# A new order of work, with all k products and w_out casts on GpSimd, in a fused linear-attention and maxout kernel

## The chip, the cores and the metric

The kernel runs on one core of one Trainium2 chip. A core has a matrix engine (TensorE, PE in the profile), three engines for elementwise work (VectorE or DVE, ScalarE or ACT, GpSimd or POOL), and a queue engine (SyncE, SP) that issues loads. Time is the device time of one execution in microseconds; the number for a kernel is the median of several runs.

## The reference

Two parts follow each other. The first is a recurrent linear attention with a decay per key channel, for 4 batches, 8 heads, 768 steps and head size 48:

```python
for t in range(S):
    state = alpha[:, :, t, :, None] * state + np.einsum('bhd,bhe->bhde', k[:, :, t], v[:, :, t])
    y[:, :, t] = np.einsum('bhd,bhde->bhe', q[:, :, t], state)
```

The result, as x of 3072 tokens by 384, goes through a maxout layer with 1024 hidden channels:

```python
h1 = x @ w1
h2 = x @ w2
g = np.maximum(h1, h2)
return (g @ w_out).astype(np.float32)
```

All inputs and the output are 32-bit floats in memory.

## The kernel before

**The mathematics as the kernel has it.** The recurrence is cut into chunks of 128 steps. In a chunk, the decay is a running sum of logarithms. ScalarE takes the logarithm of alpha (`lg`, L481), TensorE forms the running sums by a product with a triangle of ones (`cs`, L492, or L503 for the first units), and ScalarE takes exp of the sums and of their negatives (`em`, L530 and L532). k is multiplied by `em` (`kn`, L573) and q by the exponential of the sums (`qn`, L575). Both are transposed on TensorE (`tp`, L583) and copied out of PSUM (`qu` or `qk`, L588 and L593). TensorE forms the scores k times q (`pp`, L676); VectorE masks them with a triangle (`pt`, L698); y is the masked scores times v plus q times the old state (`y`, L707 and L710). The state is carried as `tm` and `sb` (L659 to L663, L634), with k times v from TensorE (`kv`, L604 or L647). y is cast (`yc`, L718), transposed (`x`, L724) and copied to `xt` (L732 and L735).

The maximum of two products is rewritten: max(h1, h2) = relu(x(w1 - w2)) + x w2. So the kernel forms w12 = w1 - w2 (L460, VectorE, in four pieces) and w2o = w2 w_out (L440 transposes of w2, L450 products, L454 copies), both once. For a unit it computes relu(x w12) (`hp` and `gt`, L765 and L776) and then x w2o + relu(...) w_out (`op`, L796), copies it out of PSUM (`os`, L804) and stores it. All products take 16-bit operands. w_out is cast to 16 bits (`wo16`, L465) in four pieces of 128 x 768; a piece holds two of the eight blocks of 128 hidden channels, and every one of the three L450 sums needs all eight.

**Units.** A unit is 256 steps of one batch, two chunks; there are 12 units, unit u being batch u mod 4, and steps 256 (u div 4) onward. The function `gla` records the first part of a unit and `moe` the second, `weights` and `w2_rows` the work on the weights. Units 0 to 2 hold their steps in an interleaved layout (`TWO`), the others in plain order.

**What sets the order.** Nothing is executed when it is recorded. `Plan.add` records an operation with its engine, an estimated length in us, what it reads and writes, and a key. `Plan.schedule` then lays all operations on the engines by simulating them: at each moment an engine takes, of the operations that are ready and whose PSUM banks are free, the one with the lowest key. Keys are 10 times the unit plus an offset; `PRI` adds to single operations' keys, and `KEY_...`, `JOIN_...` to kinds of them. The order that results is then emitted, each engine running its own part in that order. The estimated lengths have no effect on the chip but through that order. Where TensorE has a gap of over 0.15 us in the first 40 us of the plan, products of a zero tile (`wsrc`, L471) are emitted as filler. A group that uses a part of TensorE's rows (L492, L604, L676) is marked `tiled`, and has its own key (`join`) when the group before it was tiled as well.

**Loads.** SyncE issues all loads. `HEAD` gives their order at the start: a, k, q, v with a number are the four inputs of that unit, w2 and w1 with a number are thirds and quarters of w2 and w1, wo with a number are quarters of w_out (the four pieces). From unit 2 on the loads follow unit by unit.

Of the kernel before, what the change touches and what calls it, by code (L numbers as in the profile page):

```python
# [184 lines left out]


KEY_W12 = 8
KEY_W = 3
KEY_WO = 21
KEY_M = 20  # L190
CAPS = {'g': 6, 'm': 5, 'w': 3}
W12_POOL = ()
WT_ACT = (0,)
WO_ACT = (2, 3)
RELU_DVE = 99
TM_ACT = 2
X_LAST = 0
LATER = 0.75
# [2 lines left out]
TWO = (0, 1, 2)  # L201
MERGE = 3
COMBO = 99
JOIN_CS = -2
JOIN_PP = -50
CS_UP = 2
RING = 3
PAIR = 2
PAIR_ON = 'DVE'
W2_ON = ('A', 'A', 'P')  # L210
XT_ACT = ()
QU_ACT = (1,)
KN_DVE = (0,)
VX_DVE = (0,)
PRI = {'PE:op.1.1.0@1': 10, 'PE:op.0.0.0@0': 15.0, 'PE:op.1.0.0@1': 3, 'PE:op.0.1.0@0': 4.5, 'DVE:tm.4.1@3': -33.5, "POOL:('vx', 2).1@2": -16.5, 'PE:hp.1.1@1': -3.0, 'PE:cs.4.0@4': -10, 'POOL:kn.1@6': -5, 'POOL:sb.0.0@4': 12, 'PE:hp.3.3@3': 1.5, 'ACT:qu.0.1@0': -13.5, 'PE:hp.4.1@4': 5.0, 'DVE:pt.1.1@5': 5, 'PE:pp.0.1.0@0': -15, 'DVE:pt.0.0@0': 9, 'PE:y.5.0@5': 10.5, 'PE:hp.5.1@5': 13.5, 'DVE:tm.2.1@3': -9, 'ACT:cs.7.0@7': 5, 'PE:op.4.1.0@4': 9, 'DVE:tm.2.1@4': -11, 'PE:y.0.0@0': 5, 'DVE:pt.0.1@3': 10, 'PE:cs.2.0@2': -9, 'DVE:tm.3.1@5': 9, 'ACT:cs.7.1@7': -5, 'PE:hp.2.3@2': -3, 'PE:pp.1.0.0@1': 3}
HEAD = 'a0 a1 k0 q0 v0 q1 k1 w20 w22 v1 w21 wo0 wo1 wo2 w13 w10 wo3 w11 w12'


@with_exitstack
def kernel(  # L220
# [51 lines left out]
    GT = sbt("gt", [128, NF, 2 * C], FP16, 3)  # L272
    OS = sbt("os", [128, 2, DM], FP32, 3)
    VX = sbt("vx", [128, 3, H, D], FP16, max(1, len(TWO)))
    QU = sbt("qu", [128, 2, 2, HP, 2, 64], FP16, 2)
    w2f, w1f = (LD[i].rearrange("p a x -> p (a x)").rearrange("p (s f) -> p s f", s=ND) for i in (4, 5))
    wof = LD[6].rearrange("p a x -> p (a x)").rearrange("p (s d) -> p s d", s=NF)
    w2h, = sbt("w2h", [128, ND, DFF], FP16)
# [15 lines left out]

    def two(t):
        return t.rearrange("p (h r d) -> p r h d", r=2, h=H)

    P = Plan()
    P.pri, P.u = PRI, None
# [8 lines left out]
    def b16(x, n):  # L308
        return bank(x)[:, :].bitcast(FP16)[:, 0:n]
# [65 lines left out]
        )  # L375
    add("POOL", c_u, 0.6, writes=["u16"], key=KEY_T2)
    for i in range(RING):
        add("DVE", lambda i=i: nc.vector.memset(KN[i][:, :, D:64], 0.0), 0.17, writes=[("kn", i)], key=-6)
        add("DVE", lambda i=i: nc.vector.memset(QN[i][:, :, D:64], 0.0), 0.17, writes=[("qn", i)], key=-5)
    for i in range(2):  # L380
        add("DVE", lambda i=i: nc.vector.memset(LS[i][:, :, D:64], 0.0), 0.17, writes=[("ls", i)], key=KEY_T2)
    for i in range(4):
# [74 lines left out]
    def weights(g):  # L457
        fs = slice(256 * g, 256 * g + 256)
        eng, ns = ("POOL", nc.gpsimd) if g in W12_POOL else ("DVE", nc.vector)
        add(eng, lambda: ns.tensor_sub(out=w12[:, :, fs], in0=w1f[:, :, fs], in1=w2f[:, :, fs]),  # L460
            1.9 if g in W12_POOL else 0.95, reads=[("w1f", g), *(("w2f", ds) for ds in range(ND))],
            writes=[("w12", g)], key=KEY_W12)
        on = g in WO_ACT
        cp = nc.scalar.copy if on else nc.gpsimd.tensor_copy
        add("ACT" if on else "POOL", lambda: cp(  # L465
            out=wo16[:, 2 * g : 2 * g + 2, :], in_=wof[:, 2 * g : 2 * g + 2, :]),
            0.73 if on else 0.9, reads=[("wof", g)], writes=[("wo16", g)], key=KEY_W)

    def busy(n, b):
        for _ in range(n):  # L470
# [67 lines left out]
    def gla(u):  # L538
        P.u = u
        n, by2 = u % NLD, u in TWO  # L540
        k0 = 10 * u
        de, cp = DE[u % 8], u // B
        if u == 0 or u - 1 < max(COMBO, MERGE):
# [20 lines left out]
        def prep(i):  # L564
            ci = 2 * u + i
            kk, m3 = k0 + 2 + 2.5 * i, ci % RING
            kn, qn = KN[m3], QN[m3]
            kin = two(KF[n])[:, i] if by2 else nat(KF[n])[:, i]
            qin = two(QF[n])[:, i] if by2 else nat(QF[n])[:, i]
            rk = [("kf", n, x) for x in ((0, 1) if by2 else (i,))]  # L570
            rq = [("qf", n, x) for x in ((0, 1) if by2 else (i,))]
            on, ns = ("DVE", nc.vector) if ci in KN_DVE else ("POOL", nc.gpsimd)
            add(on, lambda: ns.tensor_mul(out=kn[:, :, 0:D], in0=kin, in1=EM[m3]),  # L573
                0.55 if on == "DVE" else 0.97, reads=[*rk, ("em", m3)], writes=[("kn", m3)], key=kk)
            add("DVE", lambda: nc.vector.tensor_mul(out=qn[:, :, 0:D], in0=qin, in1=csv(u, i)),  # L575
                0.5, reads=[*rq, ("cs", u, i)], writes=[("qn", m3)], key=kk)
            tp = ("tp", u, i)
            P.ps(tp, 1, "g")
            for w, (src, key) in enumerate(((qn, ("qn", m3)), (kn, ("kn", m3)))):
                def e_tp(w=w, src=src):  # L580
                    t = b16(tp, 1024).rearrange("p (w j c) -> p w j c", w=2, j=HP)
                    for j in range(HP):
                        nc.tensor.transpose(t[:, w, j, :], pm(src[:, 2 * j : 2 * j + 2, :]), ident)  # L583
                add("PE", e_tp, 0.222, reads=[key, "ident"], writes=[tp], key=kk)
            if by2:
                on = ci in QU_ACT
                cp = nc.scalar.copy if on else nc.vector.tensor_copy
                add("ACT" if on else "DVE", lambda: cp(  # L588
                    out=qu[:, :, :, :, i, :].rearrange("p a w j c -> p (w j) a c"),
                    in_=b16(tp, 1024).rearrange("p (y a c) -> p y a c", a=2, c=64)),  # L590
                    1.0 if on else 0.65, reads=[tp], writes=[("qu", TWO.index(u) % 2, i)], key=kk)
            else:
                add("DVE", lambda: nc.vector.tensor_copy(  # L593
                    out=QK[m3], in_=b16(tp, 1024).rearrange("p (w j c) -> p w j c", w=2, j=HP)),
                    0.6, reads=[tp], writes=[("qk", m3)], key=kk)
                add("POOL", lambda: nc.gpsimd.tensor_copy(out=VC[ci % 4], in_=nat(VF[n])[:, i]),  # L596
                    0.48, reads=[("vf", n, i)], writes=[("vc", ci % 4)], key=kk)
# [12 lines left out]
        def chunk(a):  # L610
# [5 lines left out]
            for x in (kvp, yp, xp, *pp):  # L616
                P.ps(x, 1, "g")
            if by2:
                qt = [qu[:, a, w].rearrange("p j r c -> p j (r c)") for w in range(2)]
                rqk, vc, rv, um, ru = [("qu", TWO.index(u) % 2, 0), ("qu", TWO.index(u) % 2, 1)], vx[:, 2 * a], [(vk, x) for x in range(4)], u2, "u2"  # L620
            else:
                qt = [QK[m3][:, w] for w in range(2)]
                rqk, vc, rv, um, ru = [("qk", m3)], VC[m4], [("vc", m4)], u16, "u16"
# [14 lines left out]
            if more:  # L638
                if by2:
                    if a == 0:  # L640
                        P.ps(("kv", u, 1), 1, "g")
                        add("PE", kv2, 0.35, reads=[("kn", (2 * u) % RING), ("kn", (2 * u + 1) % RING), (vk, 0), (vk, 1)],
                            writes=[("kv", u, 0), ("kv", u, 1)], key=kk + 0.1, tiled=True)
                else:
                    def e_kv():
                        for j in range(HP):
                            nc.tensor.matmul(  # L647
                                b32(kvp, DM)[:, 96 * j : 96 * j + 96], lhsT=pm(KN[m3][:, 2 * j : 2 * j + 2, :]),
                                rhs=pm(vc[:, 2 * j : 2 * j + 2, :]), start=True, stop=True,
                            )  # L650
                    add("PE", e_kv, 0.168, reads=[("kn", m3), ("vc", m4)], writes=[kvp], key=kk + 0.1)
                tmi = P.tm_next(u % B)
                for h2 in range(2):
                    r, e = slice(64 * h2, 64 * h2 + 64), slice(D * h2, D * h2 + D)
# [12 lines left out]

            qts[a] = (qt, pp, rqk)

            def e_p(which):  # L670
                for w in which:
                    qt, pp, _ = qts[w]
                    for j in range(HP):
                        for e in range(2):
                            r = slice(64 * e, 64 * e + D)
                            nc.tensor.matmul(b32(pp[e], 512)[:, C * j : C * j + C], lhsT=qt[1][r, j, :],  # L676
                                             rhs=qt[0][r, j, :], start=True, stop=True)
            if u < MERGE:
                add("PE", lambda: e_p((a,)), 0.215, reads=rqk, writes=pp, key=kk, tiled=True, join=kk + JOIN_PP)
            elif a == 0:  # L680
                for x in (("pp", u, 1, 0), ("pp", u, 1, 1)):
                    P.ps(x, 1, "g")
# [11 lines left out]
                else:  # L694
                    add("PE", lambda: e_p((0, 1)), 0.43, reads=rd, writes=wr, key=k0 + 4.5, tiled=True, join=k0 + 4.5 + JOIN_PP)
            uv = um.rearrange("p r c -> p (r c)") if by2 else um
            for e in range(2):
                add("DVE", lambda e=e: nc.vector.tensor_mul(  # L698
                    out=pt[:, e], in0=b32(pp[e], 512).rearrange("p (j c) -> p j c", j=HP),
                    in1=uv.unsqueeze(1).to_broadcast([128, HP, C])),  # L700
                    0.6, reads=[pp[e], ru], writes=[("pt", m3, e)], key=kk)

            def e_y():
                t = b32(yp, DM)
# [7 lines left out]
                            start=not has, stop=(e == 1) or not has,  # L712
                        )
            add("PE", e_y, 0.378 if has else 0.21,
                reads=[*rqk, ("pt", m3, 0), ("pt", m3, 1), *rv] + ([("sb", m4, 0), ("sb", m4, 1)] if has else []),
                writes=[yp], key=kk)
            yc = YC[ci % 2]
            add("ACT", lambda: nc.scalar.copy(out=yc, in_=b32(yp, DM)),  # L718
# [171 lines left out]
```

## Time and profile before

| | us |
|---|---|
| median of 8 runs | 138.03 (137.86 to 138.21) |
| the profiled execution | 138.12 |
| span of the profiled execution | 136.4 |

The span reaches from the first instruction of the program to the end of the last. Busy time of the engines and what TensorE's time is made of, by the page:

| engine or group | busy us | share or count |
|---|---|---|
| TensorE | 130.9 | 96% |
| VectorE | 91.0 | 67% |
| ScalarE | 91.0 | 67% |
| GpSimd | 65.4 | 48% |
| filler on TensorE (L471) | 10.4 | 122 products |
| k products on GpSimd (L573) | 22.7 | 23, mean 1000 ns |
| relu on ScalarE (L776) | 28.3 | 48, mean 599 ns |

In a row for a group the line comes first, then engine, operation, what is written and read, the shapes, and the count; then busy time, the mean length of one in ns, and how long the engine idled just before these and what released it. Products on TensorE are pipelined: the length of one is about twice the interval at which they follow each other, so the interval is what counts. In the chain of waits each row is a start, a length, and an engine with a line.

### The profile page before, as it was taken

Reading aid. Unit: us, or ns where it says so; the run is one execution under the profiler, and the core shown is the slowest. Engines: PE = TensorE matmul, PEld = TensorE weight load, DVE = VectorE, ACT = ScalarE, POOL = GpSimd, SP = SyncE. Lnnn points to the kernel's source line nnn. Section 1 sums busy time; section 2 is a strip of 40 time slices with the busy share of each in tenths; the row PEclk is TensorE's granted clock in tenths of the full one; section 3 lists DMA queues with packets and bytes.
Section 4 is the critical chain, followed back from the end, with each engine's and each line's share of the span. In section 5 each row is a group of like instructions: output and inputs, shape, how many; then the busy total and the mean of one; then the engine's idle time right before and its main releaser. Section 6 shows DMA issues by size and latency. Waiting matters only on the chain.

```text
span 136.4 us, 4240 instructions
## 1 busy us (share of the span) xinstructions
PE 130.9 (96%) x1669; PEld 101.6 (75%) x1669; DVE 91.0 (67%) x201; ACT 91.0 (67%) x189; POOL 65.4 (48%) x126
## 2 busy tenths in 40 slices
PE   6999799999999999999999999999999999999990
PEld 6888676777668777777877778777778778777870
DVE  4589797823899878967789489566758657572000
ACT  3695785899856957865846667568749468264640
POOL 7464874007593484470780873743747619300000
PEclk9999999999999999999999999999999999999999
DMA  4999999999999999989999989999999030030202
GB/s 98 325 327 386 390 366 358 292 247 265 213 210 241 249 217 251 276 163 191 285 184 248 280 190 265 243 233 262 213 194 244 6 115 0 5 115 0 107 26 103
DMA packets 84179, 28.58 MB, mean 210 GB/s; under 512 B 78400, under 2 KB 83392, under 8 KB 84160
## 3 DMA queue, kind: packets, MB, share of 16 engines
q1 hardware_dynamic: 81120, 23.60, 72.3%
q10 hardware_dynamic: 3040, 4.72, 9.4%
q8 instruction: 13, 0.21, 0.6%
q14 instruction: 6, 0.05, 0.1%
HBM read 23.59 MB, written 4.72 MB: 208 GB/s over the span
## 4 chain that ended last, share of the span: by engine, by line
PE 81%; SPq 9%; DMA 6%; ACT 1%; issue 1%; ACTq 0%
PE pb L796 31%; PE pb L765 23%; PE pb L583 7%; DMA ld<-in_moe_w_out_dram 6%; SPq L393 5%; PE pb L676 4%; SPq L421 3%; PE pb L710 3%; PE pb L724 3%; PE pb L707 2%; PE pb L492 2%; PE pb L450 2%; PE pb L647 2%; PE pb L525 1%; ACT wo L465 1%
## 5 line engine op out<-in xcount | busy, mean ns | idle before, releaser
L573 POOL TENSOR_TENSOR kn<-ld,em 128x384 f16<-128x384 f32 x23 | 22.7, 1000 | 34.9 <-ACT em L530 27.3
L796 PE MATMUL pb<-wo,gt 128*128 128x384 f16 (+2 forms) x200 | 39.2, 319 | 0.0
L765 PE MATMUL pb<-xt,w 128*128 128x256 f16 x288 | 35.6, 272 | 0.0
L776 ACT ACTIVATE gt<-pb 128x512 f16<-128x512 f32 x48 | 28.3, 599 | 8.5 <-PE pb L765 7.6
L698 DVE TENSOR_TENSOR pt<-pb,u 128x512 f16<-128x512 f32 x48 | 30.0, 682 | 5.9 <-PE pb L676 5.4
L765 PEld LDWEIGHTS <-w 128*128 128x128 f16 x288 | 27.0, 98 | 4.4 <-issue 0.6
L634 POOL TENSOR_TENSOR sb<-tm,dd 64x192 f16<-64x192 f32 x40 | 20.2, 506 | 10.7 <-DVE tm L659 5.2
L796 PEld LDWEIGHTS <-gt 128*128 128x128 f16 x200 | 17.4, 98 | 8.2 <-issue 0.3
L804 ACT COPY os<-pb 128x384 f32<-128x384 f32 (+2 forms) x25 | 11.7, 466 | 16.5 <-PE pb L796 16.5
L593 DVE COPY qk<-pb 128x1024 f16<-128x1024 f16 x18 | 12.4, 689 | 7.3 <-PE pb L583 7.1
L575 DVE TENSOR_TENSOR qn<-ld,pb 128x384 f16<-128x384 f32 x24 | 12.5, 548 | 6.7 <-ACT pb L532 4.9
L796 PE MATMUL pb<-w2o,xt 128*128 128x384 f16 (+2 forms) x75 | 15.8, 319 | 0.0
L718 ACT CAST yc<-pb 128x384 f16<-128x384 f32 x24 | 11.7, 489 | 5.4 <-PE pb L710 5.4
L530 ACT ACTIVATE em<-pb 128x384 f32<-128x384 f32 x24 | 11.1, 488 | 3.6 <-PE pb L492 2.6
L659 DVE TENSOR_TENSOR tm<-pb,sb 64x192 f32<-64x192 f32 x32 | 11.3, 352 | 0.9 <-PE pb L647 0.2
L481 ACT ACTIVATE lg<-ld 128x768 f16<-128x768 f32 x12 | 10.1, 845 | 2.5 <-DMA ld<-in_alpha_dram 2.4
L471 PE MATMUL pb<-wsrc 128*128 128x128 f16 x122 | 10.4, 243 | 1.1 <-DVE wsrc L313 1.1
L532 ACT ACTIVATE pb<-pb 128x384 f32<-128x384 f32 x24 | 11.0, 486 | 0.0
L710 PEld LDWEIGHTS <-pt 128*128 128x128 f16 x192 | 9.7, 96 | 1.3
L596 POOL CAST vc<-ld 128x384 f16<-128x384 f32 x18 | 9.2, 509 | 1.9 <-DMA ld<-in_v_dram 1.3
L735 DVE COPY xt<-pb 128x384 f16<-128x384 f16 x18 | 6.3, 353 | 5.2 <-PE pb L724 4.7
L471 PEld LDWEIGHTS <-wsrc 128*128 128x128 f16 x122 | 8.8, 111 | 1.1 <-DVE wsrc L313 1.0
(86 smaller groups left out, 182.4 us busy)
## 6 DMA issues: line engine op xcount, KB each, us to landing
ld<-in_alpha_dram SPq DMA_DIRECT2D x12, 384.0 KB, 4.7
out_dram<-os ACTq DMA_DIRECT2D x11, 384.0 KB, 3.5
ld<-in_k_dram SPq DMA_DIRECT2D x18, 192.0 KB, 4.6
ld<-in_q_dram SPq DMA_DIRECT2D x18, 192.0 KB, 4.4
ld<-in_v_dram SPq DMA_DIRECT2D x18, 192.0 KB, 4.5
ld<-in_moe_w_dram SPq DMA_DIRECT2D x3, 512.0 KB, 6.6
ld<-in_moe_w_out_dram SPq DMA_DIRECT2D x4, 384.0 KB, 7.9
ld<-in_moe_w_dram SPq DMA_DIRECT2D x4, 384.0 KB, 8.7
```

The costliest lines, as they stand in the source:

```text
L471: nc.tensor.matmul(PB[b][:, 0:128], lhsT=wsrc, rhs=wsrc, start=True, stop=True)
L573: add(on, lambda: ns.tensor_mul(out=kn[:, :, 0:D], in0=kin, in1=EM[m3]), 0.55 if on == "DVE" else 0.97, reads=[*rk, ("em", m3)], writes=[( ...
L575: add("DVE", lambda: nc.vector.tensor_mul(out=qn[:, :, 0:D], in0=qin, in1=csv(u, i)), 0.5, reads=[*rq, ("cs", u, i)], writes=[("qn", m3)], ...
L593: add("DVE", lambda: nc.vector.tensor_copy(out=QK[m3], in_=b16(tp, 1024).rearrange("p (w j c) -> p w j c", w=2, j=HP)), 0.6, reads=[tp], w ...
L634: add("POOL", lambda r=r, e=e: nc.gpsimd.tensor_mul(out=sb[r, :, e], in0=TM[tmo][r], in1=dd[r, :].unsqueeze(2).to_broadcast([64, HP, D])), ...
L698: add("DVE", lambda e=e: nc.vector.tensor_mul(out=pt[:, e], in0=b32(pp[e], 512).rearrange("p (j c) -> p j c", j=HP), in1=uv.unsqueeze(1).t ...
L710: nc.tensor.matmul(t[:, 96 * j + D * e : 96 * j + D * e + D], lhsT=pt[:, e, j, :], rhs=vc[:, 2 * j + e, :], start=not has, stop=(e == 1) o ...
L718: add("ACT", lambda: nc.scalar.copy(out=yc, in_=b32(yp, DM)), 0.38, reads=[yp], writes=[("yc", ci % 2)], key=kk)
L765: nc.tensor.matmul(t[:, m, :], lhsT=w12[:, ds, f * 128 : f * 128 + 128], rhs=xt[:, ds].rearrange("p a c -> p (a c)"), start=(ds == 0), sto ...
L776: add("ACT", lambda g2=g2, v2=v2: nc.scalar.activation(out=g2, in_=v2(), func=ACTF.Relu), 0.48, reads=[x], writes=[("gt", u % 3, f2)], key ...
L796: nc.tensor.matmul(b32(x, c1 - c0), lhsT=l, rhs=r, start=first and y == 0, stop=last and y == len(ws) - 1)
L804: add("ACT", lambda m=m, x=x, c0=c0, c1=c1: nc.scalar.copy(out=os_[:, m, c0:c1], in_=b32(x, c1 - c0)), 0.06 + w / 1200.0, reads=[x], write ...
```

## The change

Constants, estimated lengths and placements change, and with them the order on all engines.

- All four casts of w_out go to GpSimd (`WO_ACT` is empty; pieces 3 and 4 were on ScalarE).
- All 24 k products go to GpSimd (`KN_DVE` is empty; chunk 0's was on VectorE).
- The copy of transposed x of chunk 1 goes from VectorE to ScalarE (`XT_ACT`).
- The relu of the second pair of hidden blocks goes from ScalarE to VectorE for units 2 to 11 (`RELU_DVE`).
- In `HEAD`, k of unit 0 now precedes alpha of unit 1, v of unit 0 precedes q of unit 0, and the last piece of w_out precedes the first piece of w1 that stood before it.
- Keys, `JOIN_CS` and the whole table `PRI` are new. The lengths assumed for the casts of w_out are 0.83 and 0.85 (were 0.73 and 0.9), that of a k product on VectorE 1.0 (was 0.55).
- Operations on a chunk can be cut into two halves by head (`HALF`). `HALF` is empty, so none is cut; the names by which operations depend on each other now carry the half.
- The tile `qu` and the transposes for it are stored with q and k next to each other for each pair of heads; sizes and counts stay.

```diff
-KEY_W = 3
-KEY_WO = 21
-KEY_M = 20
+KEY_W = 9
+KEY_WO = 16
+KEY_M = 18
...
-WO_ACT = (2, 3)
-RELU_DVE = 99
+WO_ACT = ()
+RELU_DVE = 2
...
-JOIN_CS = -2
+JOIN_CS = -5
...
-XT_ACT = ()
+XT_ACT = (1,)
 QU_ACT = (1,)
-KN_DVE = (0,)
+HALF = ()
+KN_DVE = ()
...
-HEAD = 'a0 a1 k0 q0 v0 q1 k1 w20 w22 v1 w21 wo0 wo1 wo2 w13 w10 wo3 w11 w12'
+HEAD = 'a0 k0 a1 v0 q0 q1 k1 w20 w22 v1 w21 wo0 wo1 wo2 w13 wo3 w10 w11 w12'
...
-    QU = sbt("qu", [128, 2, 2, HP, 2, 64], FP16, 2)
+    QU = sbt("qu", [128, 2, HP, 2, 2, 64], FP16, 2)
...
-            0.73 if on else 0.9, reads=[("wof", g)], writes=[("wo16", g)], key=KEY_W)
+            0.83 if on else 0.85, reads=[("wof", g)], writes=[("wo16", g)], key=KEY_W)
...
-            add(on, lambda: ns.tensor_mul(out=kn[:, :, 0:D], in0=kin, in1=EM[m3]),
-                0.55 if on == "DVE" else 0.97, reads=[*rk, ("em", m3)], writes=[("kn", m3)], key=kk)
...
+                add(on, lambda hs=hs: ns.tensor_mul(out=kn[:, hs, 0:D], in0=kin[:, hs], in1=EM[m3][:, hs]),
+                    0.53 if nh == 2 else 1.0 if on == "DVE" else 0.97,
+                    reads=[*rk, ("em", m3)], writes=ks, key=kk)
...
+                        t = t.rearrange("p (j w c) -> p w j c", w=2, j=HP) if by2 else t.rearrange("p (w j c) -> p w j c", w=2, j=HP)
...
-                qt = [qu[:, a, w].rearrange("p j r c -> p j (r c)") for w in range(2)]
+                qt = [qu[:, a, :, w].rearrange("p j r c -> p j (r c)") for w in range(2)]
```

What the new order is around the steps that matter: before, TensorE's products with pieces 1 and 2 of w_out (L450) had y of unit 1's first chunk between them, and six products with piece 4 came after two L765 groups; now y comes after the first products with piece 2, and the six come after one L765 group. On GpSimd the casts are pieces 1, 2, half of `sb` of unit 1, piece 3, the other half, piece 4. The scores of unit 3 and the sums of unit 4 stood next to each other, and now have three L765 groups between them. The relu on VectorE stands ahead of the masks of the next unit (L698).

## The prediction

> **What bounds the kernel now.** I read the page's busy shares first, then the waits, then the chain of waits, and last the timeline where the chain leaves TensorE.
>
> ```profile
> PE 130.9 (96%) x1669; PEld 101.6 (75%) x1669; DVE 91.0 (67%) x201; ACT 91.0 (67%) x189; POOL 65.4 (48%) x126
> ...
> L471 PE MATMUL pb<-wsrc 128*128 128x128 f16 x122 | 10.4, 243 | 1.1 <-DVE wsrc L313 1.1
> ```
>
> TensorE is busy nearly all the time, and 10.4 us of that is filler (L471, multiplying zeros while data is on the way). The list of TensorE's own waits holds one row between 18 and 28 us, and is empty from 22.1 to 133 us:
>
> ```profile
> PE pb L450 <- POOL wo L465: 0.3, 1, 0.3
> ```
>
> So after 22 us no other engine sets the end: only what TensorE itself has to do counts. What can be won lies before that. The chain of waits shows where it comes from:
>
> ```profile
> 12.99 8.18 DMA ld<-in_moe_w_out_dram
> 21.19 0.84 ACT wo L465
> 22.07 0.48 PE pb L450 x2
> ...
> 24.40 1.31 PE pb L765 x12
> 25.71 0.97 PE pb L450 x6
> 26.69 2.62 PE pb L765 x24
> ```
>
> Until 21 us the chain is loads, then a cast of w_out, then TensorE to the end. The timeline of that passage (start, length, engine, line, tiles):
>
> ```profile
> 19.17 1.80 POOL L465 CAST wo<-ld 128x768 f16<-128x768 f32 x2 [0.73 <-DMA ld<-in_moe_w_out_dram]
> ...
> 20.05 0.81 PE L450 MATMUL pb<-wo,w2T 128*128 128x384 f16 x4 [0.29 <-POOL wo L465]
> ...
> 20.70 0.36 PE L710 MATMUL pb<-vx,pt 128*128 128x48 f16 x8
> ...
> 20.93 1.08 POOL L634 TENSOR_TENSOR sb<-tm,dd 64x192 f16<-64x192 f32 x2
> 21.02 1.54 PE L450 MATMUL pb<-wo,w2T 128*128 128x384 f16 x7
> 21.19 0.83 ACT L465 CAST wo<-ld 128x768 f16<-128x768 f32 x1 [1.04 <-DMA ld<-in_moe_w_out_dram]
> ...
> 22.42 0.96 DVE L460 TENSOR_TENSOR w<-ld,ld 128x768 f16<-128x768 f32 x1 [0.61 <-DMA ld<-in_moe_w_dram]
> ...
> 24.41 0.83 ACT L465 CAST wo<-ld 128x768 f16<-128x768 f32 x1 [0.97 <-DMA ld<-in_moe_w_out_dram]
> ```
>
> The casts start as their loads land: 19.1, 20.1, 21.2 and 24.4 us for the four pieces of w_out; the first subtraction (L460) starts on its load at 22.4. Pieces of the weights thus land about 1.1 us apart, one place in the queue after the other, whatever they hold. I call these places slots.
>
> **The change, part by part.**
>
> *Load order.* The first seven loads change places among themselves. They serve the first unit; both orders have finished the same TensorE work (all of unit 0 up to its transposed x, the three transposes of w2, and unit 1's scores and k-v products) before the first L450, and that one waits for w_out's first piece, which keeps its slot. What the head wins or loses earlier ends in filler: 122 of them before, 131 after, at 56 ns. I count 0. The last piece of w_out moves one slot forward (24.4 to about 23.3) and w1's first piece one back (about 23.3 to 24.4).
>
> *Casts of w_out.* Two leave ScalarE (0.83 us each) for GpSimd (0.825 each by the pair at 19.17). GpSimd does pieces 1 and 2 until 20.97 as before, then half of sb (L634, 1.08 for two) to 21.50, piece 3 to 22.33, the other half to 22.9, and piece 4, landed at 23.3, by 24.2.
>
> *TensorE from the first L450 to the first product with w1's first piece.* Work in it: 24 L450 at 0.1625 (22.94 to 23.91 holds six) is 3.90; unit 1's y 0.20 and 0.37; two transposes of y at 0.17; one L765 group 0.655. Sum 5.46. Before, it ran from 20.05 to 26.03 (26.69 less the 0.655 of the L765 group that is inside x12 at 24.40 but outside this set): 5.98, so 0.52 of waiting and friction, of which 0.12 before the piece-2 products at 21.02, 0.24 before piece 3. 0.16 is friction. After: y of unit 1 no longer stands between the products of pieces 1 and 2, so TensorE, done with piece 1 at 20.70, waits until 21.02: 0.32. Piece 3 is first used at 21.02 + 0.325 + 0.20 + 6 x 0.1625 = 22.52 and is ready at 22.33: no wait. Piece 4 is used after 24.7 and is ready at 24.2: none. So 5.46 + 0.32 + 0.16 = 5.94, end at 25.99: **-0.05 us**. The next product needs w1's first piece: 24.4 + 0.96 (L460) = 25.4, hidden with 0.6 to spare. If that cover went, every later product would slip one for one.
>
> *A rule that speaks against it.* The Trainium skill (SBUF — State Buffer, "Who interferes with whom") says a VectorE operation with two SBUF inputs and a GpSimd operation that reads SBUF lock each other out. The trace agrees:
>
> ```profile
> 6.99 1.14 DVE L573 TENSOR_TENSOR kn<-ld,em 128x384 f16<-128x384 f32 x1 [1.48 <-ACT em L530]
> ...
> 9.00 0.55 DVE L556 CAST vx<-ld 64x768 f16<-64x768 f32 x1
> 9.10 1.14 POOL L556 CAST vx<-ld 64x768 f16<-64x768 f32 x1 [0.63 <-DMA ld<-in_v_dram]
> ```
>
> The k product on VectorE took 1.14 us beside GpSimd's (6.72 to 7.71), against 0.55 for the like q product (L575), and GpSimd's cast 1.14 beside VectorE's against 0.85 alone. By the rule, L460 can hold up a w_out cast that GpSimd now does, by up to 0.96. By the rows: L460 runs 22.42 to 23.38, piece 4 lands at 23.3, so it waits 0.1 at most and has 0.5 to spare. The sum stays the same by both; the bound for piece 4 is 0 to +0.46 (0.96 less the spare).
>
> *k product of chunk 0 to GpSimd* (1.14 off VectorE, 1.0 on GpSimd, L573), *one copy of transposed x to ScalarE* (0.35 off VectorE by L732; no row on ScalarE, nearest is its cast of y, L718, 0.49; between 0.35 and 0.6). GpSimd has both k products of unit 0 done two times 1.0 after the first exponential (before: 6.72), at about 8.5, and their transposes end long before the first L450, in time that is filler now; the copy is issued behind two tm copies that end at 20.7, ends before 21.3, and its reader comes after 23.4: 0. If the first is later than that shows, it is so against the 0.45 that TensorE stood before the first L450. The qu tile's new layout keeps all counts and sizes: 0.
>
> *Ten relus (second f pair, units 2 to 11) from ScalarE (0.60) to VectorE.* No row; between 0.60 (ScalarE's) and 0.68 (L698, a VectorE read of the same PSUM shape); I take 0.68, the nearer. VectorE's total becomes 91.0 - 1.14 - 0.35 + 6.8 = 96.3 us (71%). In a late unit it lies here:
>
> ```profile
> 111.36 2.48 DVE L698 TENSOR_TENSOR pt<-pb,u 128x512 f16<-128x512 f32 x4 [0.94 <-PE pb L676]
> ```
>
> VectorE idles 0.94 before this; the relu starts with the product's end at 111.1 and ends at 111.8, so the four masks end at 114.3 and not 113.84; their last reader starts at 114.74. Hidden, 0.4 to spare. The tightest place is unit 2, where the relu, after two tm, one ls and before the masks, ends at about 45.6: three masks later is 47.5, and y of unit 3 comes at 47.8. 0.3 to spare.
>
> *Order of unit 2 and 3 on TensorE.* Scores of unit 3 (L676) and sums of unit 4 (L492), side by side before, now stand three L765 groups apart. Both use part of the array. The Trainium skill (TensorEngine Tiling (Array Packing), "Key Properties") says that a change of tiling mode drains TensorE; it gives no figure. The rows give one:
>
> ```profile
> 63.52 0.55 PE pb L676 x16
> 64.08 0.33 PE pb L492 x4
> 64.40 0.19 PE pb L525 x4
> ...
> 83.70 0.08 PE pb L525 x4
> ```
>
> L676 takes 0.55 after a full-array product and 0.45 after L492 (45.59); a way out costs 0.09. One more stretch: **+0.19** by the rows; by the rule without a figure, more than nothing. The same rows show L525 at 0.19 straight after a tiled stretch and 0.08 after a full product. Straight after: five units before (4, 6, 9, 10, 11), four after (4 to 7): **-0.10**.
>
> *Tail.* From unit 11's products with w1 on, TensorE's order is the same in both: 0.
>
> Sum on the profiled execution's span: 136.4 - 0.05 + 0.19 - 0.10 = 136.4 us. The span lies 1.6 us under the median of the runs (138.03), and the profiled run took 138.12. Forecast **138.1 us**, no change.
>
> **The rivals.**
>
> *Faster.* The wait in the w_out passage closes: pieces 1 and 2 land earlier behind the new load order. For it: the chain leads back into those loads; TensorE stood 0.45 before the first L450 (19.55 to 20.05). Against: they keep their slots. It can give 0.32 + 0.2, then the product with w1's first piece (not before 25.5) stops it: 138.1 - 0.5 = 137.6.
>
> *Slower.* VectorE comes late to the masks because of the relus. Place: unit 2 with 0.3 to spare, then the other nine with 0.4. Below that delay nothing is seen; above, each unit adds the excess to TensorE. For it: ls took 0.66 instead of 0.36 once (44.58), beside a GpSimd cast. With 0.08 a unit, +0.8: 138.9. Against: VectorE is idle 29% of the time, and a unit can catch up in it.
>
> *The slot swap bites.* w1's first piece lands 0.6 later than its slot says, past 25.0; delay passes one for one, with 1.0 late: +0.4, 138.5. Against: slots are regular to 0.1.
>
> **How the numbers follow.** No change 0.42, faster 0.22, relus 0.26, slot 0.10. 0.2% (0.28 us) is about what a measurement of this kernel can tell from no change. No change gives 0.40 of its chance within 0.2% and 0.01 to each side; part of the two slower cases' small ends (0.02) and of the faster one's (0.01) fall within too: faster 0.22, same 0.43, slower 0.35. The likeliest case alone: 137.9 to 138.35. Range: down to the faster case's stop with 0.1 below it, up to the relus' case: 137.5 to 138.9.
>
> **What would show it.** First L450 at 20.0 and the next group, after a wait of about 0.3 for GpSimd, at 21.0; the L765 group on w1's first piece at 26.0 without a wait for VectorE; no row of TensorE's waits over 0.1 after 22 us; L676 of unit 3 alone at 0.55; VectorE about 96 us busy. Wrong if masks (L698 before) or qk copies release TensorE in the middle, or if the first L450 starts before 19.8.

## The result

| | before | after |
|---|---|---|
| median of the runs | 138.05 us (32 runs) | 138.59 us (12 runs) |
| ratio after/before | | 1.0033, 95% interval 1.0018 to 1.0048 |
| the profiled execution | 138.12 us | 138.83 us |
| its span | 136.4 us | 136.8 us |
| median span of all executions | 136.3 us | 136.5 us |
| run less span, median | 1.71 us (1.66 to 1.79) | 2.05 us (2.00 to 2.11) |

The change makes the kernel slower by 0.33% (0.25 to 0.66 us), more than measurement can hide. The forecast was 138.1 us, no change. Its range, 137.5 to 138.9, held the time; the interval of its likeliest case, 137.9 to 138.35, did not. The last row of the table, the time of an execution less the span of its own profile, is the surprise: some 0.34 us of the loss lie outside the profiled span, where the rows of the engines show no work. The other 0.2 us or so lie inside.

The page of the changed kernel, busy times and two groups:

```profile
PE 131.9 (96%) x1678; PEld 102.4 (75%) x1678; DVE 96.7 (71%) x209; ACT 85.1 (62%) x178; POOL 68.2 (50%) x129
...
L719 DVE TENSOR_TENSOR pt<-pb,u 128x512 f16<-128x512 f32 x48 | 29.9, 681 | 0.9 <-PE pb L692 0.7
...
L475 PE MATMUL pb<-wsrc 128*128 128x128 f16 x131 | 11.2, 248 | 1.1 <-DVE wsrc L317 1.1
```

VectorE has 96.7 us of work, where 96.3 were forecast, and stands idle for only 0.9 us ahead of the masks (L719). The list of TensorE's waits between 18 and 28 us has one row, and after that none:

```profile
PE pb L454 <- POOL wo L469: 0.2, 1, 0.2
```

The timeline of the w_out passage (start, length, engine, line, tiles):

```profile
20.14 0.81 PE L454 MATMUL pb<-wo,w2T 128*128 128x384 f16 x4
...
21.12 0.48 PE L454 MATMUL pb<-wo,w2T 128*128 128x384 f16 x2 [0.17 <-POOL wo L469]
...
22.38 0.50 POOL L650 TENSOR_TENSOR sb<-tm,dd 64x192 f16<-64x192 f32 x1
...
22.52 1.18 DVE L464 TENSOR_TENSOR w<-ld,ld 128x768 f16<-128x768 f32 x1 [0.69 <-DMA ld<-in_moe_w_dram]
...
23.52 0.86 POOL L469 CAST wo<-ld 128x768 f16<-128x768 f32 x1 [0.64 <-DMA ld<-in_moe_w_out_dram]
...
24.65 0.96 DVE L464 TENSOR_TENSOR w<-ld,ld 128x768 f16<-128x768 f32 x1
...
24.96 1.14 PE L454 MATMUL pb<-wo,w2T 128*128 128x384 f16 x6
...
25.93 2.78 PE L787 MATMUL pb<-xt,w 128*128 128x256 f16 x24
```

This is the passage as forecast: the first product with w_out at 20.1, the next pieces' products a wait later at 21.1, the last six (24.96) after a cast that ended at 24.38, and the products with w1's first piece at 25.93. From the landing of w_out's first piece to the first product of unit 0's output it takes 10.07 us (10.09 before). One execution says little of so small a difference: over the profiles of this document that leave this passage as it was, it is 10.05 to 10.10 in the changed order (six) and 10.09 to 10.30 in the order before (five).

Inside the span the two executions then part at two places only. On the same work, the changed kernel is 0.06 us later at the end of the head, 0.16 after unit 3's sums, and 0.37 from 47.6 us to the end. From the first product of unit 0's output to the end it takes 107.57 us, before 107.27, and the kernels below that leave the order of that part alone repeat both figures within 0.02 us. The loss of 0.30 there is thus no accident of one execution; as the median spans part by only 0.2, about 0.1 must be gained ahead of it (an estimate from these figures). The first place, on ScalarE and TensorE, in the kernel before:

```profile
32.40 0.50 ACT L804 COPY os<-pb 128x384 f32<-128x384 f32 x1
32.77 0.22 ACT L535 ACTIVATE de<-pb 128x16 f32<-128x16 f32 x1
...
33.95 1.06 ACT L776 ACTIVATE gt<-pb 128x512 f16<-128x512 f32 x2
35.03 0.84 ACT L481 ACTIVATE lg<-ld 128x768 f16<-128x768 f32 x1
...
36.12 0.49 PE L492 MATMUL pb<-lg,t 64*128 64x384 f16 x4
```

In the changed kernel:

```profile
32.45 0.61 ACT L798 ACTIVATE gt<-pb 128x512 f16<-128x512 f32 x1
33.26 0.18 ACT L539 ACTIVATE de<-pb 128x16 f32<-128x16 f32 x1 [0.20 <-DVE qn L590]
33.34 0.47 ACT L826 COPY os<-pb 128x384 f32<-128x384 f32 x1
...
34.76 0.58 ACT L798 ACTIVATE gt<-pb 128x512 f16<-128x512 f32 x1
35.37 0.84 ACT L485 ACTIVATE lg<-ld 128x768 f16<-128x768 f32 x1
...
36.27 0.50 PE L496 MATMUL pb<-lg,t 64*128 64x384 f16 x4
```

The logarithm of unit 3 ends at 36.21, and its sums on TensorE (L496) start at 36.27. Before, it started at 35.03 and TensorE did not wait. ScalarE does the same operations here in both kernels, in another order: one of the two relus (L776, now L798) goes first, and the exponential `de` comes after it, waits 0.20 us for VectorE's q product, and stands ahead of the copy `os` that used to precede it. TensorE's starts are 0.10 further apart for it, too little for a row in the list of waits. The second place is the extra stretch on a part of TensorE's rows, first before, then after:

```profile
45.09 0.50 PE L492 MATMUL pb<-lg,t 64*128 64x384 f16 x4
45.43 0.61 PE L676 MATMUL pb<-qk 48*128 48x128 f16 x16
45.97 0.25 PE L525 MATMUL pb<-ind,ls 128*128 128x4 f16 x4
```

```profile
44.43 0.62 PE L692 MATMUL pb<-qk 48*128 48x128 f16 x16
44.98 2.14 PE L787 MATMUL pb<-xt,w 128*128 128x256 f16 x18
47.05 0.50 PE L496 MATMUL pb<-lg,t 64*128 64x384 f16 x4
47.48 0.25 PE L529 MATMUL pb<-ind,ls 128*128 128x4 f16 x4
```

Scores (L692) and sums (L496) stand apart, as the order said, where they stood side by side before (45.09 and 45.43); 0.21 us are lost between 43 and 48 us.

### The profile page after: what moved, and what is told of

Its sections match the earlier page's. It is cut to its first block, busy times and chain, and to the rows that moved or that the text cites. A ratio compares the mean times of both kernels' runs of the same rounds, so it can differ in the third digit from the quotient of the medians.

```text
span 136.8 us, 4255 instructions
## 1 busy us (share of the span) xinstructions
PE 131.9 (96%) x1678; PEld 102.4 (75%) x1678; DVE 96.7 (71%) x209; ACT 85.1 (62%) x178; POOL 68.2 (50%) x129
## 4 chain that ended last, share of the span: by engine, by line
PE 82%; SPq 8%; DMA 5%; POOL 1%; issue 1%; ACT 0%; ACTq 0%; POOLq 0%
PE pb L818 31%; PE pb L787 24%; PE pb L597 7%; DMA ld<-in_moe_w_out_dram 5%; SPq L397 5%; PE pb L692 4%; PE pb L732 3%; PE pb L746 3%; PE pb L454 2%; PE pb L729 2%; SPq L425 2%; PE pb L496 2%; PE pb L663 2%; POOL wo L469 1%; PE pb L529 1%
## 5 line engine op out<-in xcount | busy, mean ns | idle before, releaser
L587 POOL TENSOR_TENSOR kn<-ld,em 128x384 f16<-128x384 f32 x24 | 23.7, 998 | 30.9 <-ACT em L534 21.1
L719 DVE TENSOR_TENSOR pt<-pb,u 128x512 f16<-128x512 f32 x48 | 29.9, 681 | 0.9 <-PE pb L692 0.7
L798 ACT ACTIVATE gt<-pb 128x512 f16<-128x512 f32 x38 | 22.5, 596 | 11.7 <-PE pb L787 10.6
L650 POOL TENSOR_TENSOR sb<-tm,dd 64x192 f16<-64x192 f32 x40 | 20.1, 502 | 13.6 <-DVE tm L675 7.6
L818 PEld LDWEIGHTS <-gt 128*128 128x128 f16 x200 | 16.9, 97 | 7.2 <-ACT gt L798 0.2
L475 PE MATMUL pb<-wsrc 128*128 128x128 f16 x131 | 11.2, 248 | 1.1 <-DVE wsrc L317 1.1
L475 PEld LDWEIGHTS <-wsrc 128*128 128x128 f16 x131 | 9.7, 114 | 1.6 <-DVE wsrc L317 1.0
L795 DVE TENSOR_SCALAR gt<-pb 128x512 f16<-128x512 f32 x10 | 6.9, 689 | 4.9 <-PE pb L787 4.8
```

Source lines behind the costliest of these rows:

```text
L475: nc.tensor.matmul(PB[b][:, 0:128], lhsT=wsrc, rhs=wsrc, start=True, stop=True)
L587: add(on, lambda hs=hs: ns.tensor_mul(out=kn[:, hs, 0:D], in0=kin[:, hs], in1=EM[m3][:, hs]), 0.53 if nh == 2 else 1.0 if on == "DVE" else ...
L650: add("POOL", lambda r=r, e=e: nc.gpsimd.tensor_mul(out=sb[r, :, e], in0=TM[tmo][r], in1=dd[r, :].unsqueeze(2).to_broadcast([64, HP, D])), ...
L719: add("DVE", lambda e=e, j0=j0, j1=j1: nc.vector.tensor_mul(out=pt[:, e, j0:j1], in0=b32(pp[e], 512).rearrange("p (j c) -> p j c", j=HP)[: ...
L798: add("ACT", lambda g2=g2, v2=v2: nc.scalar.activation(out=g2, in_=v2(), func=ACTF.Relu), 0.48, reads=[x], writes=[("gt", u % 3, f2)], key ...
L818: nc.tensor.matmul(b32(x, c1 - c0), lhsT=l, rhs=r, start=first and y == 0, stop=last and y == len(ws) - 1)
```

## The experiments

Each was compared with the kernel before in five rounds on one chip; four chips served in all, and on each the kernel before had a run less span of 1.70 to 1.72 us. Where the order was edited, `at` holds each operation's place in the plan, `find` lists the operations of an engine that write a tile, and the kernel is emitted in the order of `at`; nothing was planned anew.

**A stretch more per unit.** In the kernel before, the small products L525 go between scores and sums of units 4 to 11, which makes eight stretches more:

```diff
+    for u in range(4, NU):
+        cs, de = find("PE", ("cs", u, 0))
+        at[de] = at[find("PE", ("pp", 3, 0, 0))[0] if u == 4 else cs] - 1e-6
```

> The kernel before, with the four small products L525 of units 4 to 11 put between the scores (L676) and the sums (L492) that stand side by side, so that TensorE leaves and enters the part-array mode once more in each of eight units. Nothing else moves. First theory: a stretch costs 0.21 us wherever it stands (0.096 going in, 0.096 coming out, 0.01 on the first product of each kind), so +1.7 us (8 x 0.21). The prediction's own terms: 8 x 0.19 plus three more L525 straight after a stretch at 0.10, +1.8. Rival, that a stretch costs nothing by itself and the loss of the changed kernel comes from VectorE: 0.

Measured: 139.75 us, ratio 1.0132 (1.0118 to 1.0146), +1.79 us. That this is close to the +1.8 of the prediction's own terms is luck. 0.10 of it lie outside the span (run less span 1.81); from the first product of unit 0's output to the end the trace takes 1.51 us longer, which is 0.19 per stretch, and the 3 x 0.10 for L525 do not show; the rest lies ahead of that, where nothing was moved. The timeline of one:

```profile
54.11 0.62 PE L676 MATMUL pb<-qk 48*128 48x128 f16 x16
54.66 0.25 PE L525 MATMUL pb<-ind,ls 128*128 128x4 f16 x4
54.84 0.50 PE L492 MATMUL pb<-lg,t 64*128 64x384 f16 x4
55.28 0.83 PE L765 MATMUL pb<-xt,w 128*128 128x256 f16 x6
```

From the scores' start to the next L765 it takes 1.17; in the kernel before the same three groups take 0.98 (0.46, 0.42 and 0.10). The price of a stretch is real and adds up: 8 x 0.19.

**L525 away from the stretch.** In the kernel before, for the four units whose L525 follows straight on the sums (6, 9, 10, 11), one L765 group goes between. It tests the term of -0.10 of the prediction.

```diff
+    for u, nxt in ((6, ("hp", 4, 3)), (9, ("hp", 7, 3)), (10, ("hp", 8, 2)), (11, ("hp", 9, 2))):
+        at[find("PE", ("cs", u, 0))[1]] = at[find("PE", nxt)[0]] + 1e-6
```

> The kernel before, with L525 of units 6, 9, 10 and 11 moved from straight after the part-array stretch to behind the L765 group that follows; the number of stretches stays. The prediction's term (L525 costs 0.10 more straight after a stretch): -0.4 us. The other reading of the same rows (the way out of a stretch costs the same whatever comes next, and is only booked on L525): 0.0.

Measured: 138.64 us, ratio 1.0048 (1.0035 to 1.0060), +0.68 us. Both expectations missed. The timeline of unit 6:

```profile
63.77 0.49 PE L492 MATMUL pb<-lg,t 64*128 64x384 f16 x4
64.19 0.83 PE L765 MATMUL pb<-xt,w 128*128 128x256 f16 x6
64.86 0.24 PE L525 MATMUL pb<-ind,ls 128*128 128x4 f16 x4
```

From the sums' start to the next group it takes 0.42, as in the kernel before, where L525 comes next (63.91 to 64.33): the way out of the stretch costs the same ahead of L765, and nothing is saved. And L525 comes 0.66 later; the second of the two exponentials of the sums (L530), which read the PSUM tile that L525 also writes, comes 0.4 later. On the same work TensorE falls about 0.17 us further behind in each of the four units, 0.68 in all. That it is these exponentials that TensorE is late for fits the order, but was not tested by itself.

**y of unit 1 back between the pieces**, in the changed kernel. It fills the 0.34 that TensorE stood before the products of piece 2.

```diff
+    at[find("PE", ("y", 1, 0))[0]] = at[find("PE", "wq0")[2]] - 1e-6
```

> The changed kernel, with y of unit 1's first chunk put back between the products with pieces 1 and 2 of w_out, where TensorE waits 0.34 for the cast. First theory: 0.2 of work fills the wait, but the product with w1's first piece can't start before its subtraction ends (25.67 for 25.77 now), so -0.1 us there, and what unit 3's sums wait for ScalarE may take even that: -0.1 to 0. If the wait for the cast is a loss of its own: -0.2.

Measured: 138.39 us, ratio to before 1.0030 (1.0018 to 1.0042). The wait shrank to 0.13, and the passage from piece 1's landing takes 9.86, where the six profiles with the passage as it was have 10.05 to 10.10. So the wait for the cast is a loss of its own, of 0.2 us in the passage, and the subtraction did not stop the gain. The medians say the same (138.39 for 138.59), but the intervals of the two ratios overlap.

**Unit 3's logarithm ahead of a relu**, in the changed kernel:

```diff
+    at[find("ACT", ("lg", 1))[1]] = at[find("ACT", ("gt", 1, 3))[0]] - 1e-6
```

> The changed kernel, with unit 3's logarithm put ahead of the last relu of unit 1 on ScalarE. First theory: TensorE's sums of unit 3 wait 0.10 for that logarithm, so -0.1 us. If this wait is a matter of the profile's one execution: 0.0. More than -0.3 would say that ScalarE's order is the main loss.

Measured: 139.36 us, ratio 1.0103 (1.0089 to 1.0116). The sums no longer wait, but the relu that was moved back is late in their place. Its list of TensorE's waits after 18 us:

```profile
PE pb L818 <- ACT gt L798: 0.7, 1, 0.7
PE pb L454 <- POOL wo L469: 0.2, 1, 0.2
```

So around 35 us ScalarE has no slack, at 62% busy on the whole. The wait of 0.10 went, and 0.77 us in all were lost for it: this edit shows the wait, but not that the 0.10 can be had back.

**Is it TensorE's program outside the span?** The changed kernel has 131 fillers instead of 122. Eight more in the kernel before, where TensorE idles, and eight fewer in the changed one:

```diff
+        n += 8 if 14.5 < t < 15 else 0     # in the kernel before
+        n += -8 if 6 < t < 7 else 0        # in the changed kernel
```

> The kernel before, with 8 more filler products (56 ns each) in the head, at 14.8 us, where TensorE otherwise stands idle until 15.4. TensorE's program is then as long as in the changed kernel (3,366 instructions instead of 3,350); nothing else differs. In the changed kernel the run lasts 2.04 us longer than the profiled span, in the kernel before 1.70. If the length of TensorE's program makes that difference: span unchanged, run less span 2.04, +0.33 us. If the other engines' programs make it, or something else in the change: run less span 1.70, 0.0 us.

> The changed kernel, with 8 filler products fewer in its longest group of filler (39 instead of 47, near 7 us), so that TensorE's program is as long as in the kernel before (3,350 instructions). If the length of TensorE's program sets the time outside the span: run less span 1.70 instead of 2.04, so +0.2 us against the kernel before instead of +0.5. If it does not: 2.04, and the time of the changed kernel, +0.5.

Measured: 138.01 us (ratio 1.0002, 0.9991 to 1.0013; run less span 1.70), and 138.62 us (1.0052, 1.0039 to 1.0065; 2.07). TensorE's program plays no part, nor does the filler.

**The relus back on ScalarE**, in the changed kernel:

```diff
-            add("DVE", lambda g2=g2, v2=v2: nc.vector.tensor_relu(out=g2, in_=v2()),
+            add("DVE", lambda g2=g2, v2=v2: nc.scalar.activation(out=g2, in_=v2(), func=ACTF.Relu),
```

> The changed kernel with its ten relus on VectorE given back to ScalarE, at the same places of the order; all else as changed. The prediction's likeliest case: the relus on VectorE were hidden, so nothing is won inside the span (136.4 to 136.8), and where ScalarE has no room TensorE may wait for it, up to +0.5. The rival of the relus, which make the masks late: the loss inside the span goes, -0.4. For the time outside the span: 2.04 if TensorE's program sets it, nearer to 1.70 if VectorE's (295 instructions instead of 309) or ScalarE's (281 instead of 277) does.

Measured: 138.59 us, ratio to before 1.0043 (1.0031 to 1.0055), span 136.5, run less span 2.07: the changed kernel's own numbers. The relus on VectorE cost nothing, and the lengths of VectorE's and ScalarE's programs (295 instead of 309, and 281 instead of 277 instructions) do not set the time outside.

**Casts in halves**, in the kernel before:

```diff
-        add("ACT" if on else "POOL", lambda: cp(
-            out=wo16[:, 2 * g : 2 * g + 2, :], in_=wof[:, 2 * g : 2 * g + 2, :]),
+        def cast():
+            nc.gpsimd.tensor_copy(out=wo16[:, 2 * g, :], in_=wof[:, 2 * g, :])
+            nc.scalar.copy(out=wo16[:, 2 * g + 1, :], in_=wof[:, 2 * g + 1, :])
+        add("ACT" if on else "POOL", cast,
```

> The kernel before with each of the four casts of w_out cut in two: the first of its two blocks of 128 rows on GpSimd and the second on ScalarE, both at the cast's place in the order. If the casts stand on the path that sets the end, as the chain of waits says, the first product with w_out starts 0.4 earlier (19.65 instead of 20.05) and the waits before the second and third pieces shrink: -0.4 us at best, less where the loads of the pieces after it (every 1.1 us) hold it. If the loads alone set that passage: 0.0. Run less span 1.70 if TensorE's program sets it; ScalarE's is 2 and GpSimd's 3 instructions longer.

Measured: 138.35 us, ratio 1.0025 (1.0012 to 1.0037), slower. The timeline of TensorE:

```profile
19.68 0.81 PE L450 MATMUL pb<-wo,w2T 128*128 128x384 f16 x4
21.22 0.36 PE L712 MATMUL pb<-vx,pt 128*128 128x48 f16 x8 [0.72 <-ACT tm L663]
21.42 1.30 PE L450 MATMUL pb<-wo,w2T 128*128 128x384 f16 x7
```

The first product came 0.4 earlier, as expected; then y of unit 1 waited 0.72 for the copies of `tm`, which ScalarE now did behind its half of the second cast. And run less span was 1.75 to 2.00, median 1.89. That kernel's GpSimd program has 194 instructions; before has 191, the changed kernel 189.

**Is it GpSimd's program?** Memsets of a scratch column, behind GpSimd's last work, where it idles:

```diff
+    more, = sbt("more", [128, 1], FP32)
+    todo += [(1e6, i, lambda: nc.gpsimd.memset(more, 0.0)) for i in range(2)]   # or 18, or 16
```

> The changed kernel with two memsets of a scratch column added on GpSimd behind its last work, so that GpSimd's program has as many instructions as in the kernel before (191 instead of 189). Of all counts only this one is common to every kernel that so far had 2.04 us outside the profiled span (189), and to none that had less (191: 1.70, 192: 1.80, 194: 1.75 to 2.00). If GpSimd's program length sets the time outside: 1.70, so +0.2 us against the kernel before instead of +0.5, with an unchanged span of 136.5. If something else of the change does, such as the order of the loads or what it moved between engines: 2.04, +0.5.

> The changed kernel with eighteen such memsets on GpSimd behind its last work (207 instructions). The traces show fetches of 8 KB of program during the run, one of them in the half-cast kernel 1.8 us after the span's end, when GpSimd's program has just ended. If a fetch of GpSimd's program that falls behind the end makes the time outside long, sixteen more instructions bring it inside the span, where GpSimd is idle from 120 us on: 1.70 or less outside, +0.2 us or less against the kernel before. If the length plays no part: 2.04, +0.5.

> The kernel before with sixteen such memsets on GpSimd behind its last work (207 instructions instead of 191). If a fetch of GpSimd's program behind the end costs time in this kernel too, it comes inside: less than 1.70 outside, down to 1.4, so -0.3 us at best. If the time outside has another cause: 1.70 and 0.0.

| kernel | GpSimd instructions | median us | ratio to before | median span | run less span |
|---|---|---|---|---|---|
| changed | 189 | 138.59 | 1.0033 (1.0018 to 1.0048) | 136.5 | 2.05 (2.00 to 2.11) |
| changed, 2 more | 191 | 138.34 | 1.0027 (1.0010 to 1.0044) | 136.6 | 1.72 (1.67 to 1.78) |
| changed, 18 more | 207 | 138.22 | 1.0010 (0.9995 to 1.0024) | 136.5 | 1.72 (1.67 to 1.78) |
| before, 16 more | 207 | 137.98 | 0.9996 (0.9988 to 1.0004) | 136.3 | 1.71 (1.67 to 1.78) |

Two instructions that do nothing for the result, on an engine that is done over 15 us before the end, take 0.33 us off the time outside the span: the longest with them (1.78) is shorter than the shortest without (2.00). In the kernel before nothing more is to be had. Five kernels of the changed order with 189 instructions, on two chips and in the result above, have 2.04 to 2.07; no kernel with 191 has a median over 1.74. (The last three rows are of one chip, on which the kernel before has 1.72.) The added memsets also make a memset GpSimd's last work, so that the count alone is the reason is not shown. What remains of the change's loss is the span's: +0.37 us with two more and +0.14 with eighteen, by their ratios.

**Filling the wait in the kernel before.** The products that wait for piece 3 let two others go first, and a subtraction goes ahead of a state copy:

```diff
+    p = find("PE", "wq0")[4]
+    for x, i in enumerate(find("PE", "wq1")[2:4]):
+        at[i] = at[p] - 2e-6 + 1e-6 * x
+    at[find("DVE", ("w12", 0))[0]] = at[find("DVE", ("tm", 3, 1))[0]] - 1e-6
```

> The kernel before with two places of its order changed in the w_out passage: the two products of piece 2 with the middle block of transposed w2 stand before the first product of piece 3, so that TensorE works in the 0.24 it waited for piece 3's cast; and the second subtraction of w1 and w2 stands before a state copy on VectorE (23.4 to 24.4 instead of 23.8 to 24.8), so that the product that follows 0.3 earlier finds it ready. If that passage sets the end, as the chain of waits says, and its waits can be filled: -0.24 us, 137.8, span 136.05, run less span 1.70 (GpSimd's program keeps its 191 instructions). If the loads hold the passage anyway (w_out's last piece lands at 24.4 and is cast by 25.24): 0.0 to -0.1.

Measured: 137.83 us, ratio 0.9984 (0.9972 to 0.9997); span 136.1, run less span 1.73. The timeline:

```profile
20.66 1.62 PE L450 MATMUL pb<-wo,w2T 128*128 128x384 f16 x9
...
23.64 1.47 PE L765 MATMUL pb<-xt,w 128*128 128x256 f16 x12
24.28 0.83 ACT L465 CAST wo<-ld 128x768 f16<-128x768 f32 x1 [1.10 <-DMA ld<-in_moe_w_out_dram]
...
25.16 1.14 PE L450 MATMUL pb<-wo,w2T 128*128 128x384 f16 x6
```

Nine products in one row, without the 0.24 wait that was between the fifth and the sixth. TensorE then has its two L765 groups done at 24.95, and stands 0.2 for the last piece (landed at 24.25, cast by 25.11), for which it had 0.3 to spare before: the wait moved to the next load. Between the landing of that piece and the first product of unit 0's output lie 4.50 us, before 4.75; from the landing of the first piece it is 10.07 and 10.09, because the pieces of this execution landed further apart (5.57 from first to last, 5.34 in the one of before). So the filling is shown, and by the medians -0.18 us of it reaches the end; by the interval it may be as little as 0.04. It is the one kernel here whose interval lies below 1: faster than the kernel before, and so than the changed one.

## Why the prediction was right or wrong

*The number: inside the range by luck.* The forecast was no change, and by the 0.2% that the prediction set as its mark the result is slower. The range reached that far up only because of the relus that make the masks late, and they cost nothing. All the signs that it named for its likeliest case came: the first product with w_out at 20.14, the next at 21.12 after a wait for GpSimd, the products with w1's first piece at 25.93, the scores of unit 3 alone at 0.55, VectorE 96.7 us busy, and no row of waits after 22 us. None of them looked at the places where the time was lost.

*The sum against the profiled execution: wrong, and the largest miss.* "The span lies 1.6 us under the median of the runs" was taken over to the changed kernel as if it were a constant. It changes with the program: 1.71 in the kernel before, 2.05 after, back at 1.72 with two more instructions on GpSimd. That is +0.34 of the +0.54 between the medians. No step of the prediction costed it, and none of its rivals was of that kind.

*One more stretch, +0.19: right.* 0.21 in the changed kernel's trace, 0.19 per stretch when eight were added. The Trainium skill's rule (TensorEngine Tiling (Array Packing), "Key Properties") that a change of tiling mode drains TensorE and the rows agree in sign; the size came from the rows.

*L525, -0.10: wrong, a misread row.* The chain's rows book the way out of a stretch on whatever follows it: 0.19 for L525 then, 0.08 otherwise. By the starts of the products the exit costs the same 0.09 to 0.10 ahead of any group, and the kernel with L525 moved away saved nothing. The term is 0. Without it the sum would have said +0.14 and not +0.04.

*ScalarE's order, not in the sum: 0.10 missed.* The prediction asked what the relus do to VectorE, and not what the new order does to ScalarE, whose load fell (91.0 to 85.1 us busy). Its order set the logarithm of unit 3 back by 0.34, 0.10 of it more than TensorE's slack.

*The head, -0.05: right.* -0.02 by the landing of piece 1 in the two executions, somewhat more over the profiles of either order (10.05 to 10.10 against 10.09 to 10.30). The wait ahead of piece 2 was 0.34 (0.32 forecast), pieces 3 and 4 cost none.

*A cover thinner than said.* The subtraction that w1's first piece needs started at 24.65, behind its load (24.53) and a state copy, and ended at 25.61, and its product started at 25.93: 0.32 to spare, not 0.6. The subtraction before it took 1.18 instead of 0.96, beside GpSimd's half of `sb` (22.38). This is the rule on VectorE and GpSimd locking each other out (the Trainium skill, SBUF — State Buffer, "Who interferes with whom"), which the prediction applied to the cast (0.86, no loss) and not to the subtraction. In all seven profiles with the changed order it holds to the hundredth: the subtraction is longer by its overlap with `sb` less 0.14 us (0.02 for 0.16, 0.10 for 0.24, 0.22 for 0.36). Of the rows shown for that rule in the prediction, only the k product's is a case of it; VectorE's cast at 9.00 has a single input.

*The rivals.* The relus: refuted as a cause, 138.59 us is the time with them on ScalarE too. The slot swap: the piece landed at 24.53, 0.13 behind its slot, and cost nothing. The wait that closes: it stayed at 0.34.

The terms as measured give -0.02 + 0.21 + 0.10 inside and +0.34 outside, +0.63 us; the runs give +0.54 by medians, and 0.25 to 0.66 by the ratio, and the difference is about what the head gains over many executions, by the estimate above. What stays open is why GpSimd's program of 189 instructions costs 0.34 behind or ahead of the span. The traces show fetches of 8 KB of program: in the kernels with 207 instructions one starts at 116 and 120 us, when GpSimd is at its 180th to 182nd instruction; in the half-cast kernel one starts 1.8 us behind the span's end. A fetch that falls behind the end would fit, but is argued, not shown; and it is not a matter of being shorter, since 192 and 194 instructions (the kernels with more stretches, and with half casts) had 1.81 and 1.89, more than 191 had.

## What to carry to other kernels

Where a change is worth a few tenths of a us, compare run less span as well as the span: the two can move apart, and here the larger part of the loss lay where the profile has no rows. If run less span differs, a few idle instructions on an engine that has finished tell cheaply whether that engine's program has a part in it. Within the span, ask of each engine what its new order makes late, also of the one that is given less to do; and look at a bound engine's waits for work that is ready and stands behind them.

## What the runs showed of the hardware

The time outside the profiled span changes with GpSimd's program: 2.04 to 2.07 us in the kernels with 189 instructions, 1.70 to 1.74 with 191 and 1.71 to 1.72 with 207, but 1.81 with 192 and 1.89 with 194. TensorE's count (3,350 or 3,366) changes nothing. The reason is open.

One more stretch of products on a part of TensorE's rows costs 0.21 us between groups on the full array and 0.19 us where the four small products L525 part it from the next, and its way out takes the same 0.09 to 0.10 ahead of any group.

A subtraction of two SBUF tiles on VectorE (128 x 768, 0.96 us alone) that starts during a GpSimd product of 64 x 192 (0.50 us) takes longer by the overlap less 0.14 us, in seven of seven profiles.
